# Strided second token weights, one transpose for u, and a new order in an attention and mixer kernel

## The chip, the core and the metric

The kernel runs on one core of a Trainium2 chip. The core has five engines with their own instruction queues: TensorE (PE, matmuls; PEld is its weight load), VectorE (DVE), ScalarE (ACT), GpSimd (POOL) and SyncE (SP), which here only issues DMAs. Data is held in SBUF, matmuls write to PSUM, inputs and outputs are in HBM (DRAM). The metric is the time on the device of one execution, in microseconds, and the median over the executions is what counts.

## What is computed

A linear attention (Performer) over 8 batches, 8 heads, 576 positions and 64 channels a head, followed by an MLP mixer over the same 8 x 576 x 512 values. Cut to what matters:

```
phi(x) = exp(x_s @ omega.T - |x_s|^2/2 - max) / sqrt(128)     # x_s = x * 64**-0.25, 128 features
kv  = phi(k).T @ v ;  z = sum over positions of phi(k)
x   = (phi(q) @ kv) / (phi(q) @ z + 1e-6)                     # heads side by side: 576 x 512

h   = relu(x.T @ w_tok1) @ w_tok2                             # w_tok1 576x256, w_tok2 256x576
u   = x + h.T
out = u + relu(u @ w_ch1) @ w_ch2                             # w_ch1 512x1536, w_ch2 1536x512
```

Inputs and output are fp32; the kernel works in fp16 with fp32 sums.

## The kernel before

576 positions do not divide by 128. The first SM = 512 of each batch are worked as NJ = 4 blocks of 128 partitions, where block j holds positions 4p + j, so that a partition's four positions lie next to each other in DRAM. The last ST = 64 positions, the tail, go through code of their own.

Attention, for each batch b and head pair hp: `proj` multiplies the transposed q and k by omega (each head of the pair on one half of the array's rows), `proj_exp` takes the exp from PSUM on ScalarE, `k_max` (VectorE) finds each key row's maximum and multiplies v by its reciprocal (the multiply is on GpSimd, or on VectorE for keys in SWAP), `kv` sums keys times values, `num` multiplies the queries with that, `norm` divides. For the tail, `k_tail` projects the tail keys of all heads, four heads to 128 rows and two head columns wide in `bd`, `k_tail_max` (lines 305 to 323) fills the zero-padded `vz` with values, 32 rows at a time, and `kv` adds two matmuls (line 393) with `k_pt` and `vz`. `q_tail` and `num_tail` do the tail queries.

Batches 0 and 1 are loaded in natural layout and transposed on TensorE (`t_main`, `t_tail`); from batch 2 on, `cast_dram` casts q and k to fp16 copies in DRAM and `load_T` brings each back by one DMA transpose of 2304 rows of 128 values.

The mixer for batch b: `tok1` (x times w_tok1, two 128-wide blocks of the 256), relu, `tok2` for each block j (w_tok2), and u = x + h on VectorE (line 478). The four blocks need the columns 4c + j of w_tok2; `permute_w2` copies them on GpSimd from `w2raw` into the packed `w2m`, and the tail columns twice into the zero-padded `w2t`. `tok2_tail` treats the tails of two batches at once: four matmuls (line 486) of 128 weight columns each, of which half are zeros, so that batch 2n lands in partitions 0 to 63 and batch 2n + 1 in 64 to 127. Then u is needed with channels on partitions. For batches 0 and 1 `tokT` transposes it on TensorE; from batch 2 on `u_write` (line 511) writes each block, one 1024-byte row a partition, to a DRAM buffer of 512 x 512, and `load_uT` (line 518) reads it back by four DMA transposes, one for each 128 channels. The eight tails together form a ninth group, number 8. `ch1` (line 530, twelve steps a group, each four 512-column matmuls and a relu on ScalarE) and `ch2` (line 542, four steps a group, each twelve 512-column matmuls, an add on VectorE at line 551 and a store) do the channel MLP.

The order is written out by hand: a string `order` lists the steps, such as `tok2 3 0` or `load_uT 3`, and each engine gets its instructions in that order. Each engine's queue, SyncE's and GpSimd's DMA issues among them, is thus fixed by it. PSUM is split in three pools: `att_ps` (4 buffers), `kn_ps` (2), `mix_ps` (2). `SWAP` is a set of keys whose PSUM copies (or v multiplies) go to the other engine than by default: `copy_on` picks ScalarE or VectorE. `HEAT` gives extra matmuls on zeros (line 166) ahead of some steps.

```
L475   ps, w2m[:, tb, j, :], live["r1", b][:, tb, :], start=(tb == 0), stop=(tb == NT - 1)
L487   ps,
       w2t[:, tb, o, :],
       live["r1", 2 * pair + o][:, tb, :],
```

Of the kernel before, what the change touches and what calls it, by code (L numbers as in the profile page):

```python
# [17 lines left out]
def kernel(  # L18
# [17 lines left out]
    nc = tc.nc  # L36
# [36 lines left out]
    HEAT = {('kv', 0, 2): 1, ('kv', 1, 0): 3, ('kv', 1, 1): 2, ('num', 0, 0): 1, ('num', 0, 3): 1, ('num', 0, 4): 1, ('num', 0, 7): 1, ('proj', 0, 1): 1, ('proj', 1, 2): 4, ('t', 0, 0, 'q'): 3, ('t', 0, 4, 'k'): 2, ('t', 0, 6, 'k'): 4, ('t', 0, 6, 'q'): 3}  # L73
    SWAP = {('c', 'q'), ('kv', 0, 3), ('kv', 1, 0), ('r1', 0, 0), ('r1', 0, 1), ('r1', 1, 1), ('t', 0, 2, 'k'), ('t', 0, 6, 'k'), ('t', 0, 6, 'q'), ('t', 1, 0, 'k'), ('t', 1, 0, 'q'), ('t', 1, 4, 'q'), ('tt', 1, 'q'), ('uT', 0, 1), ('uT', 1, 0), ('uT', 1, 1), ('uT', 1, 2), ('uT', 1, 3), ('v', 0, 2), ('v', 1, 3), None}
# [45 lines left out]
    def load_v_tail(b):  # L120
        t = ldpool.tile([P, 4, D], FP32, name="v_tail", tag="v_tail", bufs=1)
        live["vt", b] = t
        for hh in range(4):
            nc.sync.dma_start(
                out=t[32 * hh : 32 * hh + 32].rearrange("c (g w) d -> c g (w d)", g=2),
                in_=v[b, hh::4, SM:S, :].rearrange("g (c w) d -> c g (w d)", w=2),
            )
# [65 lines left out]
    w2m = wpool.tile([P, NT, NJ, P], FP16, name="w2m")  # L193
    w2t = wpool.tile([P, NT, 2, P], FP16, name="w2t")
# [5 lines left out]
    vz = [wpool.tile([P, 4, 4, 72], FP16, name=f"vz{i}") for i in range(2)]  # L200

    for t in (w1t, bd, *vz, *xt, w2t):
        nc.vector.memset(t, 0.0)
# [9 lines left out]
    nc.tensor.transpose(om_ps, omega_nat, ident16)  # L213
    nc.vector.tensor_copy(out=bd[0:D, 0:M], in_=om_ps[0:D, :])
# [10 lines left out]

    def permute_w2(tb):
        nc.gpsimd.tensor_copy(
            out=w2m[:, tb], in_=w2raw[:, tb, 0:SM].rearrange("p (c j) -> p j c", j=NJ)
        )
        nc.gpsimd.tensor_copy(out=w2t[:, tb, 0, 0:ST], in_=w2raw[:, tb, SM:S])  # L230
        nc.gpsimd.tensor_copy(out=w2t[:, tb, 1, ST:P], in_=w2raw[:, tb, SM:S])
# [16 lines left out]
    def t_main(b, h0, n, which):  # L248
# [5 lines left out]
        if HEAT.get(("t", b, h0, which)):  # L254
            heat(att_ps([P, SM], FP32, "heat_ps"), "t", b, h0, which)
        ps = att_ps([P, n, 2, P], FP16, "t_ps")
# [10 lines left out]
    def t_tail(b, which):  # L267
        nt = live[which + "natt", b]
        ps = att_ps([P, H, ST // 2], FP16, "tt_ps")
        for h in range(H):  # L270
            nc.tensor.transpose(ps[:, h, :], nt[:, h, :], ident16[0 : ST // 2, 0 : ST // 2])
        copy_on(False, "tt", b, which)(out=live[which + "T", b][:, :, NP2:SP2], in_=ps)
# [16 lines left out]
    def k_tail(b):  # L289
        sb = live["kT", b]  # L290
        kt = apool.tile([P, H, ST // 2], FP16, name="k_tt", tag="k_tt")
        (nc.vector if b < 2 else nc.gpsimd).tensor_copy(out=kt, in_=sb[:, :, NP2:SP2])
        live["kpt", b] = apool.tile([P, 4, M], FP16, name="k_pt", tag="k_pt")
        ps = att_ps([P, 4, M], FP32, "kt_ps")
        for g in range(2):
            nc.tensor.matmul(
                ps[:, 2 * g : 2 * g + 2, :],
                kt[:, 4 * g : 4 * g + 4, :].rearrange("r h c -> r (h c)"),
                bd,
                start=True,  # L300
                stop=True,
            )
        exp(live["kpt", b], ps)

    def k_tail_max(b):
        kp = live["kpt", b]
        tmp = apool.tile([P, 4, M // 2], FP16, name="mxt", tag="mxt")
# [3 lines left out]
        mx = apool.tile([P, 4], FP16, name="kmt", tag="kmt")  # L311
        nc.vector.reduce_max(out=mx, in_=tmp, axis=AX.X)
        vs = vz[b % 2]
        for hh in range(4):
            r = slice(32 * hh, 32 * hh + 32)
            with nc.allow_low_precision(reason="fp16 operand of the matmul"):
                nc.vector.reciprocal(out=vs[r, hh, :, D], in_=mx[r])  # L317
            nc.gpsimd.tensor_tensor(  # L318
                out=vs[r, hh, :, 0:D],
                in0=live["vt", b][r],  # L320
                in1=vs[r, hh, :, D : D + 1].broadcast_to((32, 4, D)),
# [59 lines left out]
    def kv(b, hp):  # L381
# [9 lines left out]
        g, h0 = hp // 2, (hp % 2) * 2  # L391
        for w in range(2):
            nc.tensor.matmul(  # L393
                ps,
                live["kpt", b][:, 2 * g + w, :],
                vz[b % 2][:, h0 : h0 + 2, 2 * g + w, 0 : D + 1],
                start=False,
                stop=(w == 1),
            )
# [54 lines left out]
    def tok1(b, tb):  # L454
        if tb == 0:
            live["r1", b] = mpool.tile([P, NT, DM], FP16, name="r1", tag="r1")
        ps = mix_ps([P, DM], FP32, "h1_ps")
        for j in range(NJ):
            nc.tensor.matmul(  # L459
                ps, w1m[:, j, tb * P : (tb + 1) * P], live["x", b][:, j, :], start=(j == 0), stop=False  # L460
            )
        nc.tensor.matmul(
            ps, w1t[:, b % 2, tb * P : (tb + 1) * P], xt[(b // 2) % 2], start=False, stop=True
        )
        if (tb == 0) != (("r1", b, tb) in SWAP):
            nc.scalar.activation(out=live["r1", b][:, tb, :], in_=ps, func=AF.Relu)
        else:
            nc.vector.tensor_relu(out=live["r1", b][:, tb, :], in_=ps)  # L468

    def tok2(b, j):  # L470
        if j == 0:
            live["u", b] = mpool.tile([P, NJ, DM], FP16, name="um", tag="um")
        ps = mix_ps([P, DM], FP32, "ht_ps")
        for tb in range(NT):
            nc.tensor.matmul(  # L475
                ps, w2m[:, tb, j, :], live["r1", b][:, tb, :], start=(tb == 0), stop=(tb == NT - 1)
            )
        nc.vector.tensor_tensor(  # L478
            out=live["u", b][:, j, :], in0=live["x", b][:, j, :], in1=ps, op=ALU.add
        )  # L480

    def tok2_tail(pair):
        ps = mix_ps([P, DM], FP32, "htt_ps")
        for o in range(2):
            for tb in range(NT):
                nc.tensor.matmul(  # L486
                    ps,  # L487
                    w2t[:, tb, o, :],
                    live["r1", 2 * pair + o][:, tb, :],
                    start=(o == 0 and tb == 0),  # L490
                    stop=(o == 1 and tb == NT - 1),
# [3 lines left out]
    def u_transpose(src, dst, *key):  # L495
        ps = mix_ps([P, ND, P], FP16, "uT_ps")
        for db in range(ND):
            nc.tensor.transpose(ps[:, db, :], src[:, db * P : (db + 1) * P], ident16)
        copy_on(False, "uT", *key)(out=dst, in_=ps)

    def tokT(b, j):
        if j == 0:
            live["uT", b] = mpool.tile([P, ND, NJ, P], FP16, name="uT", tag="uT")
        u_transpose(live["u", b][:, j, :], live["uT", b][:, :, j, :], b, j)

    def u_write(b, j):

        if j == 0:
            live["u16", b] = dpool.tile([SM, DM], FP16, name="u16", tag="u16")
        src = live["u", b][:, j, :] if b < B else ut[j]  # L510
        nc.sync.dma_start(out=live["u16", b][j * P : (j + 1) * P, :], in_=src)

    def load_uT(b):
        if b < B:
            live["uT", b] = mpool.tile([P, ND, NJ, P], FP16, name="uT", tag="uT")
        dst = live["uT", b] if b < B else uTt
        for db in range(ND):
            nc.sync.dma_start_transpose(  # L518
                out=dst[:, db].rearrange("p j c -> p (j c)"),
                in_=live["u16", b][:, db * P : (db + 1) * P],  # L520
            )
# [17 lines left out]
    def ch2(c, j):  # L539
        ps = mix_ps([P, DM], FP32, "h2_ps")  # L540
        for cb in range(NCB):
# [3 lines left out]
                wc2[:, cb, :],  # L545
# [3 lines left out]
        o = opool.tile([P, DM], FP32, name="o_sb", tag="o_sb")  # L549
        u = live["u", c][:, j, :] if c < B else ut[j]  # L550
        nc.vector.tensor_tensor(out=o, in0=u, in1=ps, op=ALU.add)  # L551
        if c < B:
            nc.sync.dma_start(
                out=out[c, 0:SM, :].rearrange("(p j) d -> p j d", j=NJ)[:, j, :], in_=o
            )
        else:
            nc.sync.dma_start(out=out[2 * j, SM:S, :], in_=o[0:ST])
            nc.sync.dma_start(out=out[2 * j + 1, SM:S, :], in_=o[ST:P])
# [6 lines left out]
    def load_v_all(b):  # L565
# [4 lines left out]
        load_nat 1 0 4 k; load_nat 1 0 4 q; cast_qk k; load_nat 1 4 8 k; cast_qk q; t_main 0 0 2 q;  # L570
        load_nat_tail 1 k; t_main 0 2 2 q; t_main 0 0 2 k; t_main 0 2 2 k; t_tail 0 k; proj 0 0; proj_exp 0 0
        1; proj_exp 0 0 0; k_tail 0; load_v_tail 1; k_tail_max 0; proj_exp 0 0 2; t_main 0 4 2 k; proj_exp 0 0
        3; k_max 0 0; proj 0 1; proj_exp 0 1 2; proj_exp 0 1 0; load_nat 1 4 8 q; proj_exp 0 1 1; t_main 0 4 2
        q; t_main 0 6 2 k; proj 0 2; proj_exp 0 1 3; proj_exp 0 2 0; proj_exp 0 2 1; kv 0 0; k_max 0 1;
        proj_exp 0 2 2; num 0 0 0; t_tail 0 q; load_wtok; norm 0 0 0; t_main 0 6 2 q; kv 0 1; k_max 0 2; proj
        0 3; proj_exp 0 2 3; num 0 1 1; norm 0 1 1; proj_exp 0 3 0; proj_exp 0 3 1; cast_dram 2 k; proj_exp 0
        3 3; num 0 1 0; t_main 1 0 4 k; t_main 1 0 4 q; num 0 0 1; norm 0 1 0; proj_exp 0 3 2; q_tail 0; k_max
        0 3; kv 0 2; t_tail 1 k; proj 1 0; load_v 1; proj_exp 1 0 0; load_wc1 0; proj_exp 1 0 1; load_nat_tail
        1 q; norm 0 0 1; num 0 2 0; k_tail 1; t_main 1 4 4 k; norm 0 2 0; permute_w2 0; k_tail_max 1; kv 0 3;
        t_main 1 4 4 q; permute_w2 1; cast_dram 2 q; num 0 3 1; proj 1 1; norm 0 3 1; k_max 1 0; proj_exp 1 0  # L580
# [114 lines left out]
```

The softmax here doesn't subtract the row's maximum and nothing guards it: scores larger than these inputs give would overflow.

## Time and profile before

| | |
|---|---|
| median of 11 executions | 308.24 us (306.58 to 311.1) |
| the profiled execution, its own time | 308.03 us |
| its span, first to last instruction | 306.2 us |
| mean granted TensorE clock | 0.996 of full speed |
| bytes moved by DMA | 46.12 MB in 78971 packets |
| SyncE: four transposes for one uT | 5.03 to 5.49 us of its queue |
| SyncE: one u write (128 KB) | 0.33 to 0.43 us of its queue, 2.1 us to landing |
| GpSimd: w2m copies | 2 x 645 ns |

In the tables of groups a line reads: source line, engine, operation, output and inputs by name, shapes, count, then total busy us and mean ns of one, then the idle time of the engine before them and what ended it. A matmul's 379 ns is its length from first to last stage; matmuls follow each other faster than that, so the distance of their starts is what a further one costs. In the chain, each line is a stretch of the work that ended last: start, length and what it was. "SPq" is SyncE's queue.

### The profile page before, as it was taken

To read this page: it belongs to the slowest core of one execution; us is meant where nothing else is said; L and a number is where in the kernel's file an instruction comes from. 1 tells how busy PE (TensorE), PEld (TensorE's weight loads), DVE (VectorE), ACT (ScalarE), POOL (GpSimd) and SP (SyncE) were. 2 spreads that over 40 slices of the span, in tenths; PEclk is the share of its full clock that TensorE was granted. 3 is DMA by queue.
4 is the path that set the end of the run, shared out by engine and by line. 5 is a ranking of instruction groups with operands and counts; after the bars stand their busy time and mean duration, and the time that the engine had idled before them with its cause. 6 is when DMAs were issued, how large, how long until landed. Compare 5 with 4: busy or idle time off the path is not lost.

```text
span 306.2 us, 5665 instructions
## 1 busy us (share of the span) xinstructions
PE 291.2 (95%) x2180; PEld 143.5 (47%) x2180; DVE 161.4 (53%) x418; ACT 157.3 (51%) x305; POOL 79.3 (26%) x115
## 2 busy tenths in 40 slices
PE   7788898999999999999999999999999999999993
PEld 3354354455544545544454545545544444444441
DVE  5688983774588676456553468547743421021021
ACT  2779456954956447753772378437633134403500
POOL 9768612511261361114220042106200000000000
PEclk9999999999999999999999999999999999999998
DMA  8999999999969979967959997350232143433021
GB/s 157 179 200 153 173 161 225 210 182 211 273 97 231 255 130 211 293 127 150 221 129 183 252 218 204 78 150 28 82 113 73 69 104 103 55 94 78 2 103 69
DMA packets 78971, 46.12 MB, mean 151 GB/s; under 512 B 46816, under 2 KB 73824, under 8 KB 78560
## 3 DMA queue, kind: packets, MB, share of 16 engines
q1 hardware_dynamic: 68000, 31.50, 42.8%
q0 software_dynamic: 10672, 13.99, 28.4%
q8 instruction: 17, 0.28, 0.4%
q10 hardware_dynamic: 272, 0.26, 0.2%
q14 instruction: 10, 0.08, 0.1%
HBM read 35.88 MB, written 20.19 MB: 183 GB/s over the span
## 4 chain that ended last, share of the span: by engine, by line
PE 77%; DVE 8%; DMA 7%; ACT 3%; SPq 2%; POOL 1%; issue 1%; DVEq 0%; POOLq 0%
PE h_ps L530 28%; PE h_ps L542 28%; PE ht_ps L475 4%; DMA wc<-in_moe_w_ch_dram 3%; PE h_ps L459 3%; DMA uT<-u 2%; PE k_ps L338 2%; PE num_ps L414 2%; PE kv_ps L388 2%; DVE km L366 2%; PE q_ps L346 2%; DVE mx L362 1%; SPq L518 1%; PE htt_ps L486 1%; DVE xm L423 1%; PE heat_ps L166 1%
## 5 line engine op out<-in xcount | busy, mean ns | idle before, releaser
L537 ACT ACTIVATE r<-h_ps 128x512 f16<-128x512 f32 x108 | 64.7, 599 | 72.5 <-PE h_ps L530 72.3
L542 PE MATMUL h_ps<-wc,r 128*128 128x512 f16 x432 | 97.0, 379 | 0.0
L530 PE MATMUL h_ps<-uT,wc 128*128 128x512 f16 x384 | 90.7, 379 | 1.1 <-DMA wc<-in_moe_w_ch_dram 0.9
L542 PEld LDWEIGHTS <-r 128*128 128x128 f16 x432 | 41.3, 98 | 47.3 <-ACT r L537 0.3
L530 PEld LDWEIGHTS <-wc 128*128 128x128 f16 x432 | 40.1, 98 | 44.6 <-issue 2.0
L551 DVE TENSOR_TENSOR o_sb<-um,h_ps 128x512 f32<-128x512 f16 x32 | 22.0, 687 | 60.6 <-PE h_ps L542 60.5
L374 POOL TENSOR_TENSOR v_sc<-v_nat,v_sc 128x512 f16<-128x512 f32 x24 | 25.4, 1057 | 101.5 <-DVE rc L422 34.7
L275 ACT ACTIVATE k_p<-k_ps 128x512 f16<-128x512 f32 x64 | 36.9, 604 | 12.6 <-PE k_ps L338 10.0
L275 ACT ACTIVATE q_p<-q_ps 128x512 f16<-128x512 f32 x64 | 37.5, 603 | 4.5 <-PE q_ps L346 4.3
L478 DVE TENSOR_TENSOR um<-xm,ht_ps 128x512 f16<-128x512 f16 x32 | 21.5, 684 | 15.4 <-PE ht_ps L475 14.7
L423 DVE TENSOR_TENSOR xm<-num_ps,rc 128x256 f16<-128x256 f32 x64 | 27.2, 424 | 2.2
L318 POOL TENSOR_TENSOR vz<-v_tail,vz 32x256 f16<-32x256 f32 x32 | 20.3, 635 | 21.0 <-DVE vz L317 15.3
L366 DVE TENSOR_REDUCE km<-mx 128x8 f16<-128x512 f16 x32 | 22.0, 686 | 1.1
L475 PE MATMUL ht_ps<-r,w2m 128*128 128x512 f16 x64 | 18.9, 380 | 2.1 <-DVE r L468 1.0
L414 PEld LDWEIGHTS <-q_p 128*128 128x128 f16 x256 | 14.3, 98 | 13.3 <-issue 2.6
L414 PE MATMUL num_ps<-kv_sb,q_p 128*128 128x65 f16 x256 | 17.0, 194 | 1.3 <-DVE kv_sb L401 1.2
L362 DVE TENSOR_TENSOR mx<-k_p 128x512 f16<-128x512 f16 x32 | 15.3, 478 | 4.5 <-ACT k_p L275 4.2
L459 PE MATMUL h_ps<-xm,w1m 128*128 128x512 f16 x64 | 16.4, 379 | 0.1
L422 DVE RECIPROCAL rc<-num_ps 128x4 f32<-128x4 f32 x64 | 10.8, 168 | 10.5 <-PE num_ps L414 10.2
L401 ACT CAST kv_sb<-kv_ps 128x130 f16<-128x130 f32 x30 | 8.1, 272 | 13.9 <-PE kv_ps L393 13.8
L346 PE MATMUL q_ps<-qT,bd 64*128 64x512 f16 x64 | 14.4, 375 | 0.6 <-ACT q_p L275 0.3
L388 PEld LDWEIGHTS <-k_p 128*128 128x128 f16 x256 | 11.3, 98 | 6.4 <-issue 1.7
(97 smaller groups left out, 245.9 us busy)
## 6 DMA issues: line engine op xcount, KB each, us to landing
out_dram<-o_sb SPq DMA_DIRECT2D x32, 256.0 KB, 2.7
v_nat<-in_v_dram SPq DMA_DIRECT2D x12, 512.0 KB, 5.5
k<-in_k_dram POOLq DMA_DIRECT2D x6, 576.0 KB, 7.5
q<-in_q_dram POOLq DMA_DIRECT2D x6, 576.0 KB, 6.1
wc<-in_moe_w_ch_dram POOLq DMA_DIRECT2D x4, 768.0 KB, 9.5
u<-um SPq DMA_DIRECT2D x24, 128.0 KB, 2.1
v_tail<-in_v_dram SPq DMA_DIRECT2D x32, 32.0 KB, 4.4
out_dram<-o_sb SPq DMA_DIRECT2D x8, 128.0 KB, 2.3
```

What stands on the lines that cost most here:

```text
L275: nc.scalar.activation(out=out, in_=in_, func=AF.Exp, bias=0.0, scale=c_scale)
L366: nc.vector.reduce_max(out=mx, in_=tmp, axis=AX.X)
L374: (nc.vector if ("v", b, hp) in SWAP else nc.gpsimd).tensor_tensor(out=vs[:, :, 0:D], in0=live["v", b][:, 2 * hp : 2 * hp + 2].rearrange(" ...
L414: nc.tensor.matmul(ps[:, j, :], live["qp", b, hp][:, j % 2, i, j // 2, :], sb, start=True, stop=True)
L423: nc.vector.tensor_tensor(out=live["x", b][:, :, h * D : (h + 1) * D], in0=ps[:, :, 0:D], in1=rc.unsqueeze(2).broadcast_to((P, NJ, D)), op ...
L459: nc.tensor.matmul(ps, w1m[:, j, tb * P : (tb + 1) * P], live["x", b][:, j, :], start=(j == 0), stop=False)
L475: nc.tensor.matmul(ps, w2m[:, tb, j, :], live["r1", b][:, tb, :], start=(tb == 0), stop=(tb == NT - 1))
L478: nc.vector.tensor_tensor(out=live["u", b][:, j, :], in0=live["x", b][:, j, :], in1=ps, op=ALU.add)
L530: nc.tensor.matmul(ps, wc1[:, db, cb * P : (cb + 1) * P], uT[:, db].rearrange("p j c -> p (j c)"), start=(db == 0), stop=(db == ND - 1),)
L537: nc.scalar.activation(out=live["r3", c][:, cb, :], in_=ps, func=AF.Relu)
L542: nc.tensor.matmul(ps, live["r3", c][:, cb, j * P : (j + 1) * P], wc2[:, cb, :], start=(cb == 0), stop=(cb == NCB - 1),)
L551: nc.vector.tensor_tensor(out=o, in0=u, in1=ps, op=ALU.add)
```

## The change

It does the following:

- `permute_w2`, `w2m` and `w2t` go; `tok2` loads its weights straight from `w2raw` with a step of four columns, and `tok2_tail` uses 64 weight columns of `w2raw`, batch 2n into output partitions 0 to 63, batch 2n + 1 into 64 to 127, the two alternating.
- The tail keys are arranged by head pair: `kt` is a zero-padded tile of its own, `k_tail` runs four 128-column matmuls with a new plain `om2`, `vz` has one slot for each head pair, and `kv` adds one matmul for the tail. `k_tail_max` works on 64 rows at a time. `load_v_tail` takes pieces of 256 bytes.
- `u_write` writes a row as four pieces of 256 bytes, into a DRAM buffer of 2048 x 128, and `load_uT` is one DMA transpose of that.
- `tok1`, `tok2`, `tokT` and `ch2` can do half of the columns (`hf`). The order uses this for batch 0's tok1, tok2 and tokT and for the last ch2 step; in the last half one of the two stores is issued by ScalarE.
- For batch 0, `t_main` and `t_tail` take their PSUM from `mix_ps`.
- `HEAT` (27 extra matmuls to 32), `SWAP` and the whole `order` are new.

```diff
 def k_tail(b):
-    kt = apool.tile([P, H, ST // 2], FP16, name="k_tt", tag="k_tt")
-    (nc.vector if b < 2 else nc.gpsimd).tensor_copy(out=kt, in_=sb[:, :, NP2:SP2])
+    for w in range(2):
+        r = slice(w * D, (w + 1) * D)
+        (nc.vector if b < 2 else nc.gpsimd).tensor_copy(
+            out=kt[b % 2][r, :, :, w, :],
+            in_=sb[r, :, NP2:SP2].rearrange("r (g i) c -> r g i c", i=2),
+        )
...
-    for g in range(2):
+    for hp in range(NU):
         nc.tensor.matmul(
-            ps[:, 2 * g : 2 * g + 2, :],
-            kt[:, 4 * g : 4 * g + 4, :].rearrange("r h c -> r (h c)"),
-            bd,
+            ps[:, hp, :],
+            kt[b % 2][:, hp].rearrange("r i w c -> r (i w c)"),
+            om2,
...
 def kv(b, hp):
-    g, h0 = hp // 2, (hp % 2) * 2
-    for w in range(2):
-        nc.tensor.matmul(
-            ps,
-            live["kpt", b][:, 2 * g + w, :],
-            vz[b % 2][:, h0 : h0 + 2, 2 * g + w, 0 : D + 1],
-            start=False,
-            stop=(w == 1),
-        )
+    nc.tensor.matmul(
+        ps, live["kpt", b][:, hp, :], vz[b % 2][:, hp, :, 0 : D + 1], start=False, stop=True
+    )
...
 def tok2(b, j, hf=None):
-            ps, w2m[:, tb, j, :], live["r1", b][:, tb, :], start=(tb == 0), stop=(tb == NT - 1)
+            ps, w2raw[:, tb, j:SM:NJ], live["r1", b][:, tb, c], start=(tb == 0), stop=(tb == NT - 1)
...
 def tok2_tail(pair):
-    for o in range(2):
-        for tb in range(NT):
+    for tb in range(NT):
+        for o in range(2):
             nc.tensor.matmul(
-                ps,
-                w2t[:, tb, o, :],
+                ps[o * ST : (o + 1) * ST, :],
+                w2raw[:, tb, SM:S],
                 live["r1", 2 * pair + o][:, tb, :],
-                start=(o == 0 and tb == 0),
-                stop=(o == 1 and tb == NT - 1),
+                start=(tb == 0),
+                stop=(tb == NT - 1),
             )
...
 def u_write(b, j):
-        live["u16", b] = dpool.tile([SM, DM], FP16, name="u16", tag="u16")
+        live["u16", b] = dpool.tile([ND * SM, P], FP16, name="u16", tag="u16")
-    nc.sync.dma_start(out=live["u16", b][j * P : (j + 1) * P, :], in_=src)
+    nc.sync.dma_start(
+        out=live["u16", b].rearrange("(d s) c -> s d c", d=ND)[j * P : (j + 1) * P],
+        in_=src.rearrange("p (d c) -> p d c", d=ND),
+    )
...
 def load_uT(b):
-    for db in range(ND):
-        nc.sync.dma_start_transpose(
-            out=dst[:, db].rearrange("p j c -> p (j c)"),
-            in_=live["u16", b][:, db * P : (db + 1) * P],
-        )
+    nc.sync.dma_start_transpose(
+        out=dst.rearrange("p d j c -> p (d j c)"), in_=live["u16", b]
+    )
...
+def cols(hf):
+    return slice(0, DM) if hf is None else slice(hf * DM // 2, (hf + 1) * DM // 2)
...
-    ch2 7 2; ch2 7 0; ch2 7 1; ch2 7 3
+    ch2 7 2; ch2 7 1; ch2 7 0; ch2 7 3; ch2 8 3 1
```

In the order before, `load_wc1 1` (the second half of w_ch1, needed by ch1 steps 6 to 11) stands after `k_max 1 1`, the third k_max of batch 1; in the new one it stands after the second, `k_max 1 1` again. Before, the ch1 steps of group 0 begin with 0, 3, 1, 4 and then 11; in the new order with 0, 3, 5, 2, 4, 1 and then 7. At the end, `load_uT 8` now stands after the first of ch2's four steps of group 6, with three following, and `load_uT 7` after two ch1 steps of group 8, with ten following. Before, `load_uT 8` stood among the ch1 steps of group 6, and `load_uT 7` after ten of group 8's.

## The prediction

> **What bounds the kernel now.** I read the page's busy table and slices first, then the chain in order of time, then the groups by shape, and last the timelines of TensorE and of SyncE's queue.
>
> ```profile
> PE 291.2 (95%) x2180; PEld 143.5 (47%) x2180; DVE 161.4 (53%) x418; ACT 157.3 (51%) x305; POOL 79.3 (26%) x115
> PE   7788898999999999999999999999999999999993
> DMA  8999999999969979967959997350232143433021
> ```
>
> TensorE is never far from full after slice 8 (61 us), and nothing else is full there. Its busy figure overstates it, since matmuls overlap, so I take distances between starts instead. The chain shows both regimes:
>
> ```profile
> 35.15 0.94 DVE mx L362
> 36.12 0.70 DVE km L366
> 37.27 1.00 POOL v_sc L374
> 38.27 9.73 DMA wc<-in_moe_w_ch_dram
> 48.04 2.76 PE h_ps L530 x12
> ...
> 63.98 0.86 PE htt_ps L486 x4
> 64.85 2.59 PE h_ps L542 x12
> ...
> 265.04 12.95 PE h_ps L542 x60
> 277.99 10.43 PE h_ps L530 x48
> 288.43 12.96 PE h_ps L542 x60
> 301.41 0.69 DVE o_sb L551
> ```
>
> Columns are start, length, what. From 48 us on the chain is TensorE, one 512-column matmul per 216 ns (12 in 2.59 us). Before that it runs through VectorE and ScalarE, and ends in a 9.73 us transfer of the first channel weights' second half, issued by GpSimd only behind a v_sc multiply. So there are two currencies: a matmul taken away after 50 us is worth its pitch in full; before 50 us only VectorE, ScalarE and that transfer count. The waits of TensorE from 60 us to 300 us sum to 1.5 us (0.5 + 0.5 + 0.3 + 0.2), so little else is to be had there.
>
> ```profile
> L393 PE MATMUL kv_ps<-vz,k_pt 128*128 128x130 f16 x64 | 8.9, 219 | 0.2 <-POOL vz L318 0.2
> L475 PEld LDWEIGHTS <-w2m 128*128 128x128 f16 x64 | 5.0, 97 | 6.9 <-issue 5.0
> L486 PE MATMUL htt_ps<-r,w2t 128*128 128x512 f16 x16 | 4.1, 378 | 0.0
> 63.01 0.28 PE L393 MATMUL kv_ps<-vz,k_pt 128*128 128x130 f16 x2
> 63.13 0.28 PE L414 MATMUL num_ps<-kv_sb,q_p 128*128 128x65 f16 x4
> 52.94 0.38 PE L346 MATMUL q_ps<-qT,bd 64*128 64x512 f16 x2
> 53.26 0.30 PE L414 MATMUL num_ps<-kv_sb,q_p 128*128 128x65 f16 x4
> 104.64 5.27 SPq L518 DMA_TRANSPOSE uT<-u  x4
> 148.77 2.06 SPq L97 DMA_TRANSPOSE qT<-q  x1
> ```
>
> The two L393 matmuls fill 63.01 to 63.13: 57 ns or so each. The two 512-column q_ps matmuls, each on half of the array's rows, fill 52.94 to 53.26: 0.32 us, where two in turn would take 0.43. So array halves work side by side, at about 0.1 us for changing over. A transpose of 2304 rows takes 2.06 us of SyncE's queue; four of 512 rows take 5.27.
>
> [...] No strided load is in this trace; the contiguous ones must be quick, as the num matmuls follow every 30 ns (four in 0.12 us), each with a load. [...] the page counts 46816 of 78971 packets under 512 B already, and no 256-byte row written to DRAM stands alone in it.
>
> **The change, part by part**, against the profiled execution's 308.03 us (span 306.2; the median of 11 is 308.24).
>
> 1. The k tail by head pairs. Each kv step has one L393 matmul in place of two: 32 x 57 ns = -1.84 us. k_tail has four 128-column matmuls instead of two of 256, the same columns; sixteen extra instructions at an estimated few ns make +0.05. Only batches 0 and 1 (a quarter of it) lie before TensorE is full; I count the whole. On VectorE (b < 2) or GpSimd (b >= 2) there is one more kt copy (399 ns on GpSimd) against two fewer vz reciprocals (179) and two fewer GpSimd vz multiplies (635). GpSimd is at 26%; nothing.
>
> 2. Token-mixing tails. The four full matmuls of tok2_tail (0.86 us in the chain) become four on 64 array columns, ordered so that neighbours use different halves. Side by side, two rounds of 216 ns, plus 0.1 us changeover as for q_ps, plus about 0.1 us for first loads[...] (a load lasts 97 ns), are 0.65. Four times -0.2 is -0.8. Bounds: nothing exposed, -1.7[...].
>
> 3. Strided second weights. Two things go: two w2m copies (0.65 us each) and four w2t copies on GpSimd, ahead of v_sc and vz work at 27 to 32 us; and a 272 ns memset. What comes is 72 loads in strides: 56 for batches 1 to 7 and 16 for batch 0 in halves. A load lies beside the matmul ahead of it, 216 ns in most places; at today's 97 ns it is hidden. Bounds: 0, and twice 97 ns, exposed by some 90 ns before the first matmul of each of 36 steps, +3.2. I take +0.3.
>
> 4. u to DRAM in four 256-byte pieces a row, back by one transpose of 2048 rows. The 28 writes grow from 128 packets to 512; SyncE's issue of 0.33 to 0.43 us may double, 28 x 0.4 = 11 us of that queue, against (5.27 - 2.06, say 2.7) x 7 = 18 us given back. Queued behind it are output stores and the next q and k transposes. In steady state uT isn't late (no wait of L530 after 60 us), so 0. At the end, load_uT 8 has three ch2 steps ahead of its first reader (7.8 us) and load_uT 7 ten ch1 steps (8.6 us), against 2 to 3 us of issue and the 5 us landing of kT: 0, upper bound +1[...].
>
> 5. Halves for batch 0 (tok1, tok2, tokT), early transposes in the mixer's PSUM buffers, new HEAT, SWAP and order. Heat matmuls go from 27 to 32, all before ch1's second half, mostly in idle TensorE time: 0 to +1.1. I counted both orders up to what ch1 0 0 needs, with uncontended durations of the rows. TensorE's own work without heat is about equal, 18.3 and 17.8 us. VectorE has 32.4 us of work before it now, of 42.2 elapsed, and 30.9 after: transposes' evictions moved to ScalarE -1.4, the r eviction -0.7, one k_max's three operations deferred -1.3, two v_sc multiplies taken over +1.4, the rest by small items. ScalarE gets 1.9 more, and had over 12 us of idle time there. So the first ch1 should start about 1.5 us sooner. GpSimd's list before the second wc transfer is shorter by w2's 2.3 us of copies, four vz multiplies (2.5) and one v_sc, and q16 and the first wc half are issued earlier. The second half then is less late, and six ch1 steps instead of four stand before its first use; TensorE's wait there (0.9 us, plus small gaps) should mostly go. Together -2.0. Bounds: -4, and +2.5 if a wait that the lists don't show lands on the chain. What is late next is VectorE's k_max for batch 1.
>
> 6. The end. The last ch2 step is done in two halves, the last one after everything else. The closing VectorE add falls from 0.69 us to about 0.4, and 128 KB less goes out after it, on two queues: -0.3 and -0.3, so -0.6 (bounds -0.2 and -0.9).
>
> Smaller matmuls of the halves: +0.1. Sum: -1.84 + 0.05 - 0.8 + 0.3 + 0 - 2.0 - 0.6 + 0.1 = -4.8, from 308.03 to 303.2; on the median's footing 303.4. I say 303.3.
>
> **Rivals.** (a) The start gives nothing: the DMA engines are at nine tenths from the first slice to the eleventh, and the same bytes must land before ch1 can run on. For it: the 9.73 us of the wc transfer; against: it was issued late, not slow alone. 308.0 - 2.8 = 305.2.
>
> (b) The start is worse: ScalarE's extra evictions hold up the exps queued behind them, and through them k_max and kv, by 2.5 us in place of the 2.0 gained. For it: k_p and q_p activations are on the chain from 8 to 20 us; against: ScalarE's idle time there. 308.0 - 2.8 + 2.5 = 307.7, no change that can be told.
>
> (c) The other side: a strided load outlasts the matmul beside it. Place: L475's loads, all 72. Price, with a load taken at four times today's 98 ns, 392: 56 x (392 - 216) + 16 x (392 - 108) = 14.4 us, on 303.2 less its own 0.3, giving 317.3. It decides once a load takes over about 216 + 4800/72 = 283 ns. Against it: today's 97 ns[...].
>
> (d) The column halves don't run side by side (the change doing less than it says): tail +0.4 instead of -0.8, 304.5. It lies in the forecast's own range.
>
> **Chances.** About 0.5% (1.5 us) is what a measurement can tell from no change. Forecast, 301 to 305, with (d): 0.56; (a) 0.20; still more from the start (below 301) 0.04; (b) 0.11; (c), or a start worse by over 4 us: 0.09. Faster is the first three, less a sliver of (a): 0.79; same: 0.12; slower: 0.09. The range 300.5 to 307.4 leaves out some 0.04 below and 0.15 above.
>
> **What would show it.** Right: L393's count halved at the same mean; htt_ps starts in pairs a few ns apart; ht_ps steps at 0.43 us each in the chain; first ch1 near 40.7 us, no wc wait over 0.5 us; one uT transpose of 2 to 3 us; a closing add near 0.4 us. Wrong: ht_ps steps at over 0.6 us; gaps ahead of L530 put down to the u transfer; ch1 starting after 42 us.

## The result and the profile after

The changed kernel takes 303.56 us (median of 12 executions), beside 308.6 us for the kernel before on the same chip; the ratio is 0.983, with a 95% interval of 0.980 to 0.986. That is 4.5 to 6.3 us less. The profiled execution took 303.51 us (span 301.7), 4.52 less than the profiled one of before. Ratios, and differences of medians, compare undisturbed executions alone here and below (for the kernel after their median is 303.26 us), while the medians quoted as measured hold a few disturbed ones too.

The busy table and two rows of the slices of the kernel after:

```profile
PE 288.6 (96%) x2199; PEld 145.0 (48%) x2199; DVE 160.1 (53%) x414; ACT 158.7 (53%) x310; POOL 67.8 (22%) x97
PE   7789898999999999999999999999999999999995
DMA  8999699997999989689499898620243036504012
```

TensorE is as full as before and 2.6 us less busy; GpSimd is 11.5 us less busy. No other engine is busy for more than 53% of the span. The DMA row stands at 9 in many slices up to the 24th, as before, but none of TensorE's listed waits after 50 us, before or after, is for a transfer. So the bound has not moved.

The groups of the kernel after that the change touches, by shape:

```profile
L394 PE MATMUL kv_ps<-vz,k_pt 128*128 128x130 f16 x32 | 7.0, 219 | 0.1
L479 PE MATMUL ht_ps<-r,w2raw 128*128 128x512 f16 x56 | 16.6, 381 | 0.7 <-ACT r L542 0.3 <-DVE o_sb L557 0.2
L491 PE MATMUL htt_ps<-r,w2raw 128*64 128x512 f16 x16 | 2.5, 391 | 0.0
L479 PEld LDWEIGHTS <-w2raw 128*128 128x128 f16 x72 | 6.7, 115 | 6.0 <-issue 4.1
```

The key tail has half its matmuls at the same length. The four matmuls of a token tail are still four, but all 16 of them keep TensorE busy for 2.5 us, where the full ones took 4.1, and less than half of 16 times 391 ns, so they overlap. A load in strides takes 115 ns on average where the packed ones took 97; the matmuls behind it did not get longer (381 against 380 ns).

TensorE's timeline in the kernel after around the first token tail (start, length from first to last matmul, what):

```profile
62.45 0.29 PE L411 MATMUL num_ps<-kv_sb,q_p 128*128 128x65 f16 x4
62.67 0.62 PE L491 MATMUL htt_ps<-r,w2raw 128*64 128x512 f16 x4
63.29 0.59 PE L479 MATMUL ht_ps<-r,w2raw 128*128 128x512 f16 x2
```

The next step starts 0.62 us after the tail began, where it was 0.86. Single records in the trace show the four starting in two pairs, 3 to 4 ns apart within a pair and 236 to 240 ns from pair to pair; the ht_ps matmul follows 0.38 us after the second pair, against 0.216 between full matmuls. After the other three tails the next matmul starts 0.56, 0.56 and 0.76 us after the tail began (before 0.86, 0.96 and 0.94). Ahead of the first pair some 0.09 us more than the usual distance pass in three of the four.

The chain of the kernel after, from just before the first use of the second half of w_ch1, and its end:

```profile
36.31 1.00 POOL v_sc L377
37.31 11.41 DMA wc<-in_moe_w_ch_dram
48.76 1.04 PE h_ps L535 x4
...
65.59 2.59 PE h_ps L548 x12
...
286.37 11.68 PE h_ps L548 x60
```

The waits of TensorE in the kernel after (total, times, longest):

```profile
PE h_ps L535 <- DMA wc<-in_moe_w_ch_dram: 1.5, 1, 1.5
```

This is where the forecast and the profile part. The transfer was issued 0.96 us sooner (37.31, before 38.27), but took 11.41 us instead of 9.73 and landed later. TensorE, which reached its first ch1 at 41.10 us instead of 42.25, stood waiting for it for 1.5 us, where it had waited for 0.9. The sizes differ between executions. In the other six profiled kernels below that keep this start, the transfer took 8.3 to 10.9 us and TensorE waited for it in one (1.0 us, the neighbouring columns); in the three others with the old start it took 7.2 to 8.2 us, and none waited.

And the end of the kernel after, over all engines:

```profile
296.76 0.69 DVE L557 TENSOR_TENSOR o_sb<-um,h_ps 128x512 f32<-128x512 f16 x1 [1.90 <-PE h_ps L548]
298.08 0.42 DVE L557 TENSOR_TENSOR o_sb<-ut,h_ps 128x256 f32<-128x256 f16 x1 [0.62 <-PE h_ps L548]
298.53 0.47 SPq L563 DMA_DIRECT2D out_dram<-o_sb  x1
298.53 0.55 ACTq L564 DMA_DIRECT2D out_dram<-o_sb  x1
```

The closing add is 0.42 us long and the two stores leave together. From the start of the closing add to the end of the span it is 301.7 - 298.08 = 3.6 us; before, 306.2 - 301.41 = 4.8.

### The profile page after: what moved, and what is told of

It reads as the page before. It is cut to its first block, busy times and chain, and to the rows that moved or that the text cites. A ratio compares the mean times of both kernels' runs of the same rounds, so it can differ in the third digit from the quotient of the medians.

```text
span 301.7 us, 5658 instructions
## 1 busy us (share of the span) xinstructions
PE 288.6 (96%) x2199; PEld 145.0 (48%) x2199; DVE 160.1 (53%) x414; ACT 158.7 (53%) x310; POOL 67.8 (22%) x97
## 4 chain that ended last, share of the span: by engine, by line
PE 82%; DVE 8%; DMA 5%; ACT 3%; issue 1%; POOL 1%; SPq 0%; DVEq 0%; POOLq 0%
PE h_ps L548 30%; PE h_ps L535 29%; DMA wc<-in_moe_w_ch_dram 4%; PE ht_ps L479 4%; PE h_ps L461 3%; PE num_ps L411 3%; PE k_ps L341 3%; PE q_ps L349 2%; PE kv_ps L391 2%; DVE km L369 1%; DMA om_f<-in_omega_dram 1%; ACT k_p L273 1%; DVE mx L365 1%; PE h_ps L464 1%; PE htt_ps L491 1%
## 5 line engine op out<-in xcount | busy, mean ns | idle before, releaser
L548 PE MATMUL h_ps<-wc,r 128*128 128x512 f16 (+1 forms) x444 | 97.2, 373 | 0.0
L548 PEld LDWEIGHTS <-r 128*128 128x128 f16 x444 | 42.3, 98 | 46.7 <-issue 0.8
L482 DVE TENSOR_TENSOR um<-xm,ht_ps 128x512 f16<-128x512 f16 (+1 forms) x36 | 22.2, 626 | 14.3 <-PE ht_ps L479 13.8
L479 PE MATMUL ht_ps<-r,w2raw 128*128 128x512 f16 (+1 forms) x72 | 19.4, 357 | 0.7 <-ACT r L542 0.3
L411 PEld LDWEIGHTS <-q_p 128*128 128x128 f16 x256 | 13.6, 98 | 11.8 <-issue 3.7
L461 PE MATMUL h_ps<-xm,w1m 128*128 128x512 f16 (+1 forms) x72 | 16.7, 355 | 0.9 <-DVE um L482 0.7
L419 DVE RECIPROCAL rc<-num_ps 128x4 f32<-128x4 f32 x64 | 10.9, 170 | 12.2 <-PE num_ps L411 12.1
L411 PE MATMUL num_ps<-kv_sb,q_p 128*128 128x65 f16 x256 | 16.3, 194 | 0.9 <-ACT kv_sb L398 0.8
L365 DVE TENSOR_TENSOR mx<-k_p 128x512 f16<-128x512 f16 x32 | 14.1, 441 | 4.9 <-ACT k_p L273 4.7
L321 POOL TENSOR_TENSOR vz<-v_tail,vz 64x256 f16<-64x256 f32 x16 | 10.5, 656 | 15.4 <-DVE vz L320 13.1
```

What stands on the lines that cost most here:

```text
L411: nc.tensor.matmul(ps[:, j, :], live["qp", b, hp][:, j % 2, i, j // 2, :], sb, start=True, stop=True)
L461: nc.tensor.matmul(ps, w1m[:, j, tb * P : (tb + 1) * P], live["x", b][:, j, c], start=(j == 0), stop=False)
L479: nc.tensor.matmul(ps, w2raw[:, tb, j:SM:NJ], live["r1", b][:, tb, c], start=(tb == 0), stop=(tb == NT - 1))
L482: nc.vector.tensor_tensor(out=live["u", b][:, j, c], in0=live["x", b][:, j, c], in1=ps, op=ALU.add)
L548: nc.tensor.matmul(ps, live["r3", c][:, cb, j * P : (j + 1) * P], wc2[:, cb, d], start=(cb == 0), stop=(cb == NCB - 1),)
```

## The experiments

Two accounts stood against each other. A: the time went with the work taken from TensorE (key tail, paired token tails) and at the end; the new start gave about nothing. B: the new order carries the gain. Most experiments undo one part in the kernel after, or do some parts in the kernel before; two try something new at its start. "Edit" is against the kernel named.

**The old key tail in the kernel after.**

```diff
-        nc.tensor.matmul(
-            ps, live["kpt", b][:, hp, :], vz[b % 2][:, hp, :, 0 : D + 1], start=False, stop=True
-        )
+        for w in range(2):
+            nc.tensor.matmul(
+                ps,
+                live["kpt", b][:, 2 * g + w, :],
+                vz[b % 2][:, h0 : h0 + 2, 2 * g + w, 0 : D + 1],
...
```

> The changed kernel with the tail keys by four heads again, two 130-column kv matmuls a step. Theory A (the gain is TensorE work taken away, the start gave nothing): 32 matmuls of 58 ns come back, +1.9 us, 305.4. Theory B (the gain is the new order and its copies' placing, matmuls taken away only uncover waits): under +0.6, 303.6 to 304.2.

Measured: 305.59 us, ratio to before 0.993 (0.991 to 0.996); the profiled execution 305.88 us. Its group has 64 matmuls again at 219 ns. The part is worth 2.3 us by the medians and 3.3 by the ratios: 32 matmuls at 57 to 58 ns make 1.8, and the profile has a new wait of 0.8 us for a v_sc of GpSimd, whose vz work the edit brings back too.

**The token tail's loops exchanged in the kernel after**, meant to take the pairing away.

```diff
-        for tb in range(NT):
-            for o in range(2):
+        for o in range(2):
+            for tb in range(NT):
```

> The changed kernel with tok2_tail's two loops exchanged, so that neighbouring matmuls use the same half of the array's columns. Theory A, with the halves side by side: 16 matmuls in turn of 216 ns instead of pairs, about +1.2 us, 304.8, and htt starts 216 ns apart but for the one change of half. Theory B: under +0.4. If the halves never ran side by side: 0.

Measured: 305.0 us (303.39 to 309.98), ratio 0.988 (0.985 to 0.991); the profiled execution 303.39 us. The timeline of this kernel's TensorE:

```profile
62.23 0.63 PE L491 MATMUL htt_ps<-r,w2raw 128*64 128x512 f16 x4
62.85 0.59 PE L479 MATMUL ht_ps<-r,w2raw 128*128 128x512 f16 x2
```

The tail takes 0.62 us as with the loops the other way, so the edit did not do what it was meant for, and what its timed runs lost can't be put down to the pairing. The single starts again come in pairs, 6 to 7 ns apart. How two matmuls that the program puts one behind the other on the same half can show such starts, these records don't tell; the pairing had to be taken away in another way.

**The zero-padded tail weights in the kernel after**: a full set of 128 weight columns for each of the four matmuls, as before.

```diff
+    w2t = wpool.tile([P, NT, 2, P], FP16, name="w2t")
...
+            nc.gpsimd.tensor_copy(out=w2t[:, tb, 0, 0:ST], in_=w2raw[:, tb, SM:S])
+            nc.gpsimd.tensor_copy(out=w2t[:, tb, 1, ST:P], in_=w2raw[:, tb, SM:S])
...
-                    ps[o * ST : (o + 1) * ST, :],
-                    w2raw[:, tb, SM:S],
+                    ps,
+                    w2t[:, tb, o, :],
```

> The kernel after with the zero-padded tail weights w2t restored (one memset of 272 ns, four copies on GpSimd after the second wc1 load, four matmuls of 128 weight columns each in turn, each with a full set of columns), so that no two run side by side. Theory A: each of the four tails costs 0.86 us again in place of 0.62, so +0.95 us, 304.5. Rival[...]: no change, 303.5.

Measured: 304.85 us, profiled 304.85, ratio 0.986 (0.981 to 0.990). In this kernel's timeline the next step comes 0.86 us after the tail's start:

```profile
62.21 1.02 PE L496 MATMUL htt_ps<-r,w2t 128*128 128x512 f16 x4
63.07 0.59 PE L485 MATMUL ht_ps<-r,w2raw 128*128 128x512 f16 x2
```

Laid beside the kernel after matmul by matmul, the four tails cost 0.2, 0.4, 0.3 and 0.3 us more, 1.2 together. By the ratios it is 1.0 and by the medians 1.6; the two ratios' intervals overlap, so the traces carry this price. Four matmuls of 64 columns thus cost less than four of 128. That neighbours on different halves are the reason isn't shown, since the exchanged loops took no longer.

**The closing step whole, in the kernel after.**

```diff
-    1; ch2 8 3 0; ch1 7 7; ...
-    3; ch1 7 4; ch2 7 2; ch2 7 1; ch2 7 0; ch2 7 3; ch2 8 3 1
+    1; ch2 8 3; ch1 7 7; ...
+    3; ch1 7 4; ch2 7 2; ch2 7 1; ch2 7 0; ch2 7 3
```

> The changed kernel with the last ch2 step of group 8 whole and in its place, so that a whole step of group 7 closes. Theory A: the closing, last matmul's start to the end of the span, goes from 4.2 us back to the 5.4 of before, +1.2 us, 304.8. Rival: only the add is shorter, +0.3.

Measured: 303.53 us, ratio 0.985 (0.983 to 0.988), profiled 303.12 us (span 301.3). Its closing add:

```profile
297.15 0.69 DVE L557 TENSOR_TENSOR o_sb<-um,h_ps 128x512 f32<-128x512 f16 x1 [1.90 <-PE h_ps L548]
```

From there to the end is 301.3 - 297.15 = 4.15 us, 0.5 more than in the kernel after, too little for the medians to show. This execution had the better start. The kernel before, with the same closing step, needed 4.8, and before with another u path, below, 305.4 - 300.93 = 4.5. In the ten profiled kernels with the halved step it is 3.6 to 3.8. Beside the kernel after the half step is thus worth 0.5 to 1.2 us; why a whole step's end differs so much between executions is open.

**The second token weights as neighbouring columns, in the kernel after.**

```diff
-                ps, w2raw[:, tb, j:SM:NJ], live["r1", b][:, tb, c], start=(tb == 0), stop=(tb == NT - 1)
+                ps, w2raw[:, tb, j * P : (j + 1) * P], live["r1", b][:, tb, c], start=(tb == 0), stop=(tb == NT - 1)
```

> The changed kernel with tok2's weights read as 128 neighbouring columns in place of every fourth: h of a block belongs to other positions than x, nothing else differs. Theory A (strided loads stay beside a matmul): 0 to -0.3 us, load mean 97 ns in place of 115. Rival (strided loads are exposed): -1.5 us or more, with shorter ht steps.

Measured: 303.27 us, ratio 0.981 (0.977 to 0.985), profiled 303.24. The loads of this kernel:

```profile
L479 PEld LDWEIGHTS <-w2raw 128*128 128x128 f16 x72 | 5.7, 97 | 6.6 <-issue 4.4
```

97 ns instead of 115, 1.0 us less of load work, and 0 to 0.3 us less in time, which this measurement can't tell from nothing: the strides are hidden.

**The old u path in the kernel after**: 1024-byte rows, four transposes.

```diff
-        nc.sync.dma_start_transpose(
-            out=dst.rearrange("p d j c -> p (d j c)"), in_=live["u16", b]
-        )
+        for db in range(ND):
+            nc.sync.dma_start_transpose(
+                out=dst[:, db].rearrange("p j c -> p (j c)"),
+                in_=live["u16", b][:, db * P : (db + 1) * P],
+            )
```

> The changed kernel with u written as 1024-byte rows and read back by four transposes, as before. Theory A (uT is never what TensorE waits for): within 0.4 us of the changed kernel, 303.2 to 304.0. Rival (the single transpose shortens waits that this order would have): +1.5 us or more, with waits of ch1 on the u transfer.

Measured: 303.96 us, ratio 0.983 (0.978 to 0.988); profiled 304.96, with one wait of 0.4 us for a uT. The ratio is that of the kernel after, so in the new order no worth of the u path can be told; by the medians it is 0.6 us, by the profiled pair 1.4, of which the wait explains 0.4.

**The new tails in the old order**: the kernel before with the key tail, the paired token tails and the halved closing step, the old u path, the old start.

```diff
-        ch2 8 3; ch1 7 0
+        ch2 8 3 0; ch2 6 1; ch1 7 0
...
-        ch1 7 8; ch2 6 1;
+        ch1 7 8;
...
-        ch2 7 1; ch2 7 3
+        ch2 7 1; ch2 7 3; ch2 8 3 1
```

> The kernel before, with its own order, u path, w2 copies, HEAT and SWAP, and three things of the change: tail keys by head pair, paired tok2_tail, the last ch2 step in halves (ch2 6 1 moved ahead of ch1 7 0 for its buffer). Theory A: the whole gain, -4.3 us from before, ratio 0.986. Theory B: the order carries it, so -1.5 or less, ratio 0.995 or more.

Measured: ratio 0.996 (0.993 to 0.998), 1.4 us gained; profiled 306.93 us. Account A, which had 4.3, fell short by two thirds. TensorE's waits in this kernel have a new first entry:

```profile
PE h_ps L538 <- DMA uT<-u: 2.9, 1, 2.9
```

SyncE's queue in this kernel has the four transposes behind that wait:

```profile
102.34 0.87 SPq L562 DMA_DIRECT2D out_dram<-o_sb  x2
103.26 7.80 SPq L526 DMA_TRANSPOSE uT<-u  x4
```

TensorE came to ch1 of group 2 some 2 us sooner and stood there for 2.9 us. In the kernel before the same four transposes were issued from 104.64 on (5.27 us of the queue). There the transfer landed only just in time; it is part of the chain that ended last:

```profile
108.65 7.12 DMA uT<-u
115.81 0.38 PE h_ps L530
```

TensorE had reached this ch1 at 114.90, and lost no more than 0.3 us before the matmul at 115.81. In the kernel with the new tails it was there at 113.08, and the matmul that waited starts at 116.80. So of the 2.9 us some 1.8 are the saved work, given back at the next transfer in line; 1.0 is a later landing: the transposes held the queue for 7.80 us in this execution, in the kernel before for 5.27.

**The same with the new u path, and the new u path alone in the kernel before.** The edit is the diff of the u path of two paragraphs up, the other way round.

> Before's order with the new tails, the paired token tails, the halved closing step, and now also the new u path (256-byte pieces, one transpose). Without the u path this order gained 1.4 us only, and its trace had a wait of 2.9 us for a uT. Theory A' (the removed TensorE work is given back at the u transfer as long as that takes four transposes): the wait goes or falls under 1 us, and the gain is 3.5 to 4.3 us, 304.0 to 305 beside a before of 308.3 (ratio about 0.987). Rival B' (the old order is held by its start and by other waits, the new order carries the gain): it stays at 306 to 307 (ratio 0.993 to 0.996), and a wait of another name stands where the uT wait was.

> The kernel before with the new u path alone. Before, TensorE does not wait for uT by more than tenths. Theory A': no gain of its own, 0 to -0.5 us (308). Rival (the u path's shorter SyncE queue, 5.3 us down to 2.2 us a time, lets other transfers come earlier and is worth over 1 us): 307 or less. If 256-byte pieces hurt: 308.5 or more.

Measured: with the tails and the u path 304.79 us, ratio 0.986 (0.982 to 0.991), profiled 304.94, a gain of 4.2 us by the ratio. No wait for a uT transfer is left, and one transpose issue stands where four were:

```profile
104.31 4.13 SPq L529 DMA_TRANSPOSE uT<-u  x1
```

The u path alone: ratio 0.997 (0.994 to 1.001), profiled 307.26, 0.8 us less than the profiled execution of before. So tails alone give 1.4, the u path alone 0.8 by the ratio with an interval that holds nothing at all, and both 4.2: the parts don't add up. By the ratios this is only just clear of the noise; that the 2.9 us wait goes with the second part says why: the second frees what the first saves. Account A names what saves the time, and left out a condition for it.

The new order meets this condition too. With the old u path it had 0.983 (the old u path in the kernel after), where the old order with the tails and the same u path had 0.996. Its transposes stand ahead of the output stores that came first in the old order, at 102.34 above. SyncE's queue in the new order with the old u path:

```profile
100.84 5.71 SPq L521 DMA_TRANSPOSE uT<-u  x4
106.66 1.66 SPq L557 DMA_DIRECT2D out_dram<-o_sb  x3
```

So either the new u path or the new order is enough, and account B was right in that the order can do it. These two kernels differ in the strided weights, HEAT, SWAP and the start as well, so that the place of the transposes is the cause is read from the traces, not tried alone. The new order with all of it is a further 1.4 us faster by the profiled executions (303.51 against 304.94), which the two ratios' intervals don't tell apart. TensorE's listed waits after 50 us are 2.1 us in the old order with tails and u path, and 0.5 in the kernel after.

**The second half of w_ch1 loaded earlier, in the kernel after.**

```diff
-        load_wc1 1; ch1 0 2;
+        ch1 0 2;
...
-        cast_dram 2 q;
+        cast_dram 2 q; load_wc1 1;
```

> The changed kernel with the second wc1 load issued right after the cast of q for batch 2, some 13 us earlier on GpSimd's queue. Theory S1 (the start is held by the late issue of that load): the 1.5 us wait goes and the time falls by 1.2 to 2 us, 301.6 to 302.4. Theory S2 (the start is held by the rate of the DMA engines): the load lands at about the same time or other loads land later, 0 to +1 us. Theory S3 (held by the chain of VectorE and ScalarE): the wait goes, but the work behind it waits elsewhere, -0.4 to 0.

Measured: 303.01 us (302.21 to 304.18), ratio 0.981 (0.977 to 0.985), profiled 302.66 us. In GpSimd's queue of this kernel the load is issued 12 us sooner:

```profile
25.30 0.77 POOL L231 DMA_DIRECT2D wc<-in_moe_w_ch_dram  x1 [0.91 <-DMA w2raw<-in_moe_w_tok_dram]
```

The wait for wc is gone from the list of waits, and the total falls by 0.3 us by the medians and by 0.9 in the profiled pair, not by 1.5. Issued 12 us sooner, the transfer took 15.7 us and landed 7.7 us sooner. The chain of this kernel no longer has the transfer in it; it runs through VectorE up to the first ch1:

```profile
38.96 0.68 DVE um L482 x2
39.67 0.20 DVE rct L442
39.89 0.44 DVE xt L443
...
41.25 0.30 DVE uT L507
41.59 3.71 PE h_ps L535 x16
```

This version was the fastest of all by its median, though its interval overlaps that of the kernel after.

**No heat matmuls in the kernel after.**

```diff
-    HEAT = {('kv', 0, 2): 5, ('kv', 1, 0): 1, ...}
+    HEAT = {}
```

> The kernel after without any of the 32 heat matmuls (they work on zeros and their result is read by nothing). Theory S (they lie in TensorE's idle time before 45 us): no change within 0.5 us. Rival H1 (they are on TensorE's path at the start, up to 32 x 216 ns of it): 0.5 to 2 us faster. Rival H2 (they keep the granted clock up at the start): slower by 0.5 us or more, with a lower PEclk in the first slices.

Measured: profiled 303.25 us, ratio 0.984 (0.975 to 0.992), an interval too wide to tell half a per cent; the profile has to do. The granted clock of this kernel by slices:

```profile
PEclk9557999999999999999999999999999999999999
```

In the second to fourth slice (7.5 to 30 us) TensorE was granted 0.5 to 0.7 of its speed, where the kernel after has 9 in every slice, and the time did not move by more than executions differ: TensorE's speed isn't what the start waits for. Neither a cost of the heat matmuls nor a gain from them is seen in the time.

## Why the prediction was right, and where it wasn't

303.3 us was forecast, 303.56 came. That the sum held is luck in good part: the start was taken far too large, and the token tails, the strided loads and the end came out better than allowed for.

1. The key tail, -1.84 + 0.05: the count halved at the same 219 ns, and undoing it cost 2.3 to 3.3 us, a new wait for GpSimd among them. Right.

2. The token tails, -0.8: 0.56 to 0.76 us, 0.62 in the mean, where 0.65 was estimated; -0.24 x 4 = -0.95 by the first tail, 1.2 by laying the traces side by side. Right in size, and rival (d)'s price of +0.4 didn't come. From the second pair to the next matmul 0.31 to 0.51 us passed, where 0.22 to 0.31 passed after the last of the four full ones; what fills that time isn't shown, and that first loads would take 0.1 us was the author's estimate. The reason given, neighbours on different halves, isn't shown.

3. The strided loads, +0.3: 115 ns instead of 97, under the 216 ns beside them, and no loss. The kernel before has no strided load, so what a stride would cost a load was the author's estimate. It was not free for the load itself, 18 ns each, but with neighbouring columns the time was only 0 to 0.3 us less, so it is hidden. Rival (c), deciding from 283 ns, was far off. The small-scale bound (exposed loads, +3.2) didn't come either.

4. The u path, 0. One transpose came as forecast, 1.7 to 3.5 us, median 2.1, and u writes took 0.46 us of issue against 0.40, not doubled. In the new order no worth other than 0 can be told. But the reason given, that uT isn't late today, was a statement about today's TensorE, and too generous even there: in the kernel before one uT landed at 115.8 with no slack left. With the tails' work gone, the old path was late by 2.9 us in the old order. A part priced at zero was thus needed for terms 1 and 2 to count there, and in the changed kernel the new order would have done without it. The forecast didn't see that the slack of a transfer shrinks by what is saved ahead of it, here by some 1.8 us.

5. The start, -2.0. This is the term that failed. The first half of it came: ch1 began 1.15 us sooner (1.5 forecast). The other half, "the second half then is less late", did not: issued 0.96 us sooner, the transfer took 1.7 us longer (11.41 against 9.73), and its wait grew from 0.9 to 1.5 us. To set a price on the whole, take every distance between matmul starts before 50 us, less the usual distance of its shape, and count heat as idle: 24.9 us of TensorE's time went unused before, 24.7 after, so 0.2 us was gained. Such a figure differs between executions: 24.1 to 25.1 in the four with the old start, 23.1 to 25.1 in the seven with the new one, means 24.7 and 24.2. The first half is smaller in the mean, too: the first ch1 begins at 42.1 to 43.1 in the four and at 41.1 to 43.1 in the seven, means 42.6 and 41.8, and the transfer was issued 0.6 us sooner and took 1.5 longer. So about half a microsecond, which the spread of either group exceeds, near rival (a)'s nothing and far from rival (b)'s loss. Rival (a)'s reason, that the DMA engines are nearly full up to the eleventh slice (9 in the row from the second on before, 6 to 9 in the kernel after), fits the longer transfer, but was not tried by itself: loading wc sooner brought only 0.3 to 0.9 us, since VectorE's chain is what is late next. The forecast did name VectorE, but the last stretch before ch1 is um, rct, xt and uT work and not batch 1's k_max.

6. The end, -0.6: -1.2 in the two profiled executions. With three whole ends of 4.2 to 4.8 us and halved ones of 3.6 to 3.8, the half step is worth 0.5 to 1.2; how much of this pair's figure is scatter of the whole end, and what makes that scatter, is open.

For the profiled pair the measured terms are -1.9 (key tail, by 32 pitches), -1.0, 0, 0, -0.2 and -1.2, together -4.3 of the 4.5 us, against -4.8 forecast.

## What to carry to other kernels

When the bound engine loses work, ask of each transfer that it consumes how much slack is left: a part that is worth nothing alone can be what lets another part count, so undo parts one at a time in the new kernel and also add them one at a time to the old. When a part turns out to be a condition, ask what else would meet it. A transfer issued earlier need not land earlier by as much: here 1 us sooner became 0.7 later, and 12 us sooner became 7.7 sooner. Look at what is late next before counting the wait as gained. And a sum that comes out right isn't evidence for its terms.

## What the runs showed of the hardware

A stride of four fp16 elements made a weight load 115 ns long instead of 97; without it the kernel took 0 to 0.3 us less, which can't be told from nothing. Four matmuls on 64 columns each took 0.56 to 0.76 us up to the start of the next one, where four on 128 took 0.86 to 0.96; the first of these tails took 0.62 us with the loops in either order. One DMA transpose of 2048 rows held SyncE's queue for 1.7 to 3.5 us in the kernel after, 2.1 in the median, and for 4.1 once in the old order; four of 512 rows held it for 5.0 to 5.5 us in six of the seven groups of the kernel before, and for 7.8 in the seventh. Writing u in 256-byte pieces instead of 1024-byte rows took 2.4 us to landing instead of 2.1, both in the median. A granted clock of 0.5 to 0.7 from 7.5 to 30 us left the time as it was, to within what executions differ by.
